# The PSUM bank of the transposes joined with the three of the channel mixing into one ring of four, with new order lists, in a fused sliding-window attention and channel-mix kernel

## The chip, the cores and the metric

The kernel runs on one core of one Trainium2 chip. The metric is the device time of one execution in microseconds (us), the median of several runs. Each order list below belongs to one engine of that core: PE (the matrix engine), DVE (the vector engine), ACT (the scalar engine), POOL and SP, which in this kernel mostly issue transfers.

## The reference

Attention over a sliding window of 128 tokens with a linear distance bias, for 8 batches, 8 heads, 576 tokens and head size 64, followed by a channel mix over the 512 joined head columns:

```python
scores = scale * np.matmul(q, k.transpose(0, 1, 3, 2))
bias = slopes[:, None, None] * (-np.abs(rel).astype(np.float32))[None, :, :]
mask = (rel >= 0) & (rel < window)              # rel = query - key, window = 128
scores = np.where(mask, scores + bias[None], -1000000000.0)
attn = softmax(scores)                          # over the keys
x = np.matmul(attn, v)                          # heads joined: (8, 576, 512)
xk = mu_k * x + (1.0 - mu_k) * x_prev           # x_prev: x one token earlier
xr = mu_r * x + (1.0 - mu_r) * x_prev
k = np.maximum(xk @ w_k, 0.0)                   # w_k: 512 x 1024
v = k * k @ w_v                                 # w_v: 1024 x 512
r = 1.0 / (1.0 + np.exp(-(xr @ w_r)))           # w_r: 512 x 512
return r * v
```

Inputs and output are float32; the kernel multiplies in bf16 and accumulates in float32.

## The kernel before

**Tiling.** The unit of the attention is a pair of heads of one batch: 32 pairs, numbered `it` = 0 to 31, four to a batch. The unit of the channel mix is two batches (1152 tokens) cut into chunks: four chunks for the first two batches, three (512, 384 and 256 tokens) for each later two. All of it is one program of small steps. A step is registered by `op(...)` with its engine, its inputs and the ring from which it takes a buffer.

**Steps of a pair.** `ct.it` (DVE) puts q and k of the pair in token order. `tq.it` (PE) transposes them into PSUM, and `pq.it` (ACT) copies them out. `score.it.h` (PE, halves h = 0 and 1) multiplies, `exp.it.h` (ACT) takes the exponential, `mask.it.h` (DVE) applies window and bias. `av.it` (PE) multiplies by v, `norm.it` (DVE) divides, `ot.it` (PE) transposes the result, `xt.it` (ACT) copies it out. `xk.it` and `xr.it` (DVE) mix it with the token before.

**Steps of a chunk**, for two batches P and a start column c0 or a row block c: `m1.P.c0.fo` (PE, product with w_k), `rl` (ACT, maximum with 0), `kk` (DVE or ACT, square), `m3.P.c` (PE, product with w_r), `rs.P.c` (ACT, gate), `m2a.P.c` and `m2.P.c` (PE, two halves of the product with w_v), `oo.P.c` (DVE, gate times value), `st.P.c` (SP, store).

**Loads.** POOL issues nearly all loads, one after the other: `lql.b...` (q and k of batches 0 to 3), `lvs.b.j` (v of batch b, five pieces; pairs 4b to 4b+3 need all of them), `lts.b.i` (the last 64 tokens of q and k), `lqn.b.i.j` (q and k of batches 4 to 7; i = 0 is q, i = 1 is k). A load also waits until the load eight issues earlier has landed.

**Batches 4 to 7** are not transposed on PE. SP issues a transposing transfer `tr.b.0` (q) and `tr.b.1` (k) from the loaded tile to `qt_buf`, and `trt.b.0`, `trt.b.1` for the last 64 tokens. There is a single `qt_buf`: the transfers of batch b must wait until all scores of batch b-1 have read it. The first half of a pair's scores needs both `tr`, the second half both `trt` as well. `lqn` of batch 6 overwrites the tile that the `tr` of batch 4 read, and `lqn` of batch 7 that of batch 5.

**PSUM.** The pools are opened in lines 65 to 67: `p_sa` (2 buffers of 2 banks: scores, and av from pair 4 on), `p_tp` (1 bank: all `tq` and `ot`), `p_mm` (3 banks: `m1`, `m3`, `m2a`/`m2`, and in the first batch the small products). A PE step that takes a buffer waits until the step that empties the previous content of that buffer is done: an ACT copy for `tq` and `ot`, `rl`, `rs` or `oo` for the others.

**Order.** A planner (`plan`) would choose the order by priorities, but the table `ORDER` fixes it: one list of step names for each engine, each engine runs its list from first to last, and a step that is not ready blocks everything behind it on that engine. The same holds for the loads in POOL's list and for the transfers in SP's.

Of the kernel before, what the change touches and what calls it, by code (L numbers as in the profile page):

```python
# [9 lines left out]
BF16 = mybir.dt.bfloat16  # L10
# [6 lines left out]
def kernel(  # L17
# [136 lines left out]
    def qk_transp(it, t0, t1, pool, tag):  # L154
        cs = T["cs", it]
        tp = T["tp", it, t0] = pool.tile([128, 1024], BF16, tag=tag, name="tp")
        for n in range(NF * t0, NF * t1):
            nc.tensor.transpose(  # L158
                tp[:, 128 * (n - NF * t0):128 * (n - NF * t0) + 128],
                cs[:, n // NF, n % NF].rearrange("p h d -> p (h d)"), ident)  # L160
# [105 lines left out]
    def x_transp(it, t0=0, t1=NJ):  # L266
        xu = T.pop(("xu", it, t0))
        tp = T["xt", it, 128 * t0] = p_tp.tile([128, 1024], BF16, tag="tp", name="tp")
        for t in range(t0, t1):
            nc.tensor.transpose(  # L270
                tp[:, 128 * t:128 * t + 128], xu[:, t].rearrange("p h d -> p (h d)"), ident)
# [177 lines left out]
    RINGS = {"sa": 2, "tp": 1, "mm": 3, "ct": 3, "xu": 3, "dl": 4, "xm": 3, "xk": 2, "rl": 3,  # L449
# [77 lines left out]
    def add_pair(it):  # L527
# [9 lines left out]
        if b == 0:  # L537
# [38 lines left out]
        else:  # L576
# [7 lines left out]
            op(("tq", it), "PE", 450, lambda: qk_transp(it, 0, 2, p_tp, "tp"), war, n, "tp",  # L584
# [17 lines left out]
        if b == 0:  # L602
            for e, (t0, t1) in enumerate(((0, 2), (2, NJ))):
# [6 lines left out]
                   [], n, "tp", uses=[("norm", it, e)])  # L610
# [22 lines left out]
        op(("ot", it), "PE", 290, lambda: x_transp(it), [], n, "tp", uses=[("norm", it)])  # L633
# [88 lines left out]
    for i, m in enumerate(FILL):  # L722
# [9 lines left out]
            m1.0.256.5 m1.0.256.4 tq.6 m1.0.256.7 av.4 score.6.0 m1.0.256.1 ot.4 av.5 score.6.1
            tq.7 m3.0.2 m3.0.1 m1.0.256.2 ot.5 score.7.1 score.7.0 tail.2 m1.0.0.7 m3.0.0 tq.8
            av.6 m3.0.3 av.7 tq.9 m2a.0.0 m2a.0.1 ot.6 score.8.1 score.8.0 m2a.0.3 ot.7 m2.0.0
            m2.0.1 score.9.1 score.9.0 m2.0.3 m1.0.512.0 tq.10 m1.0.512.4 m1.0.512.1 m1.0.512.2
            av.8 m1.0.512.5 m2a.0.2 score.10.1 score.10.0 m1.0.512.7 ot.8 m2.0.2 av.9 tq.11
            m1.0.512.6 m1.0.512.3 m3.0.4 score.11.1 score.11.0 m3.0.8 ot.9 m3.0.6 m3.0.5 tq.12
            m1.0.768.0 av.10 m1.0.768.1 tq.13 m1.0.768.2 m1.0.768.7 score.12.0 score.13.0 m2a.0.4
            tail.3 ot.10 av.11 m2.0.4 tq.14 score.12.1 m2a.0.5 score.14.1 tq.15 m2.0.5 score.13.1
            score.14.0 m1.0.768.3 ot.11 m1.0.768.5 av.12 m1.0.768.4 m1.0.768.6 score.15.0  # L740
            score.15.1 m3.0.7 ot.12 av.13 m1.1.0.0 av.14 score.17.0 m1.1.0.7 score.18.0 score.16.1
            m2a.0.6 score.18.1 m2.0.6 score.17.1 m2a.0.7 av.15 score.16.0 m1.1.0.5 ot.13
            score.19.1 score.19.0 m2a.0.8 m2.0.7 ot.14 m2.0.8 m3.1.1 ot.15 m1.1.0.1 m1.1.0.6
            m3.1.0 m3.1.2 m1.1.0.4 m3.1.3 av.17 m1.1.512.0 av.16 m1.1.0.2 m1.1.512.7 m1.1.0.3
            m1.1.512.4 m1.1.512.3 ot.16 av.18 av.19 m2a.1.2 m2a.1.3 ot.17 m2a.1.0 m2.1.2 m2.1.0
            m2.1.3 ot.18 m2a.1.1 score.21.1 score.20.0 ot.19 m2.1.1 score.22.1 m1.1.512.5
            m1.1.512.2 score.20.1 m3.1.4 m1.1.896.0 score.23.1 score.22.0 m3.1.6 m3.1.8 m1.1.512.6
            m1.1.512.1 score.21.0 score.23.0 m3.1.5 m1.1.896.2 m3.1.7 av.20 m2a.1.6 m1.1.896.6
            m2.1.6 ot.20 av.21 m1.1.896.4 m1.1.896.7 m2a.1.5 av.22 m2a.1.4 m2.1.5 ot.21 m2.1.4
            m1.1.896.3 m1.2.0.0 m1.1.896.1 m1.2.0.4 m1.2.0.1 m1.2.0.3 m1.1.896.5 m1.2.0.7 ot.22  # L750
            av.23 m3.2.0 m1.2.0.5 m1.2.0.2 m3.2.1 ot.23 m2a.1.8 m1.2.0.6 score.27.1 score.24.1
            m2.1.8 m3.2.2 score.25.0 score.26.0 m2a.1.7 m2a.2.0 score.26.1 score.25.1 m2.1.7
            m2a.2.1 score.24.0 score.27.0 m2.2.0 m2.2.1 m1.2.512.0 m3.2.3 m1.2.512.7 m1.2.512.6
            m1.2.512.5 m2a.2.3 av.24 m2a.2.2 m2.2.3 m3.2.6 m2.2.2 av.25 ot.24 m1.2.896.0 m3.2.4
            m1.2.512.2 m1.2.512.3 m1.2.512.4 av.26 m1.2.896.6 m1.2.896.7 m1.2.512.1 ot.25
# [6 lines left out]
            m1.3.512.7 m3.3.4 m3.3.8 m1.3.512.5 m1.3.512.4 m1.3.512.6 m1.3.512.3 m1.3.896.0 m3.3.7
            m1.3.896.7 m3.3.5 m1.3.896.2 m2a.3.5 m2a.3.4 m2.3.5 m2.3.4 m1.3.896.1 m3.3.6
            m1.3.896.3 m1.3.896.6 m1.3.896.5 m2a.3.6 m1.3.896.4 m2.3.6 m2a.3.8 m2.3.8 m2a.3.7
            m2.3.7
# [230 lines left out]
```

## Time and profile before

| what | value |
|---|---|
| time, median of 3 runs (lowest to highest) | 238.65 us (238.22 to 239.57) |
| span of the profiled execution, first to last instruction | 237.9 us |
| PE busy | 223.9 us (94%) |
| DVE busy | 193.2 us (81%) |
| ACT busy | 165.7 us (70%) |
| POOL busy | 93.2 us (39%) |
| mean granted clock of PE | 1.000 |

The profile gives the span of its own execution, and no device time for it. The three runs lie 0.3 to 1.7 us above that span, their median 0.75 us: this is what lies around the instructions. Busy time of PE counts each matmul from its start to its modelled end, so a matmul that streams in 216 ns may be listed with 380. DMA rows give the time from issue to landing.

### The profile page before, as it was taken

How to read it: one execution, taken by the hardware profiler on the slowest of the kernel's cores; microseconds unless marked ns; L12 is line 12 of the kernel's file. 1: busy time of each engine (PE TensorE's matmuls, PEld its weight loads, DVE VectorE, ACT ScalarE, POOL GpSimd, SP SyncE). 2: the span in 40 equal slices, each digit the busy share in tenths (PEclk: the TensorE clock that was granted, in tenths of full speed). 3: DMA queues.
4: the chain of work that ended last, by engine and by line, in shares of the span. 5: the costliest groups of instructions: out<-in, count | busy, mean ns of one | idle time of the engine just before them, and what ended most of it. 6: DMA issues, size and time to landing. Idle time of an engine off the chain costs nothing.

```text
span 237.9 us, 5426 instructions
## 1 busy us (share of the span) xinstructions
PE 223.9 (94%) x2130; PEld 132.9 (56%) x2163; DVE 193.2 (81%) x406; ACT 165.7 (70%) x281; POOL 93.2 (39%) x131
## 2 busy tenths in 40 slices
PE   6798888999999699999999999999999999999994
PEld 2355675757666465556455655445675455545573
DVE  3869999999979689998889897689669989993252
ACT  4397799978999789785299448875578974407340
POOL 8999567568646378407876610000000000000000
PEclk9999999999999999999999999999999999999999
DMA  6999999999999999999999999627220300203024
GB/s 131 166 137 184 178 160 200 188 159 210 202 139 149 134 164 135 125 123 212 193 171 184 123 123 181 193 77 148 99 90 3 118 19 0 91 0 132 0 91 178
DMA packets 114810, 31.56 MB, mean 133 GB/s; under 512 B 99160, under 2 KB 110432, under 8 KB 114784
## 3 DMA queue, kind: packets, MB, share of 16 engines
q0 software_dynamic: 89808, 16.52, 107.2%
q1 hardware_dynamic: 24976, 14.69, 29.7%
q8 instruction: 17, 0.28, 0.5%
q14 instruction: 9, 0.07, 0.1%
HBM read 33.56 MB, written 9.44 MB: 181 GB/s over the span
## 4 chain that ended last, share of the span: by engine, by line
PE 76%; DVE 13%; DMA 3%; ACT 3%; issue 2%; POOL 1%; POOLq 0%; DVEq 0%
PE pv L351 23%; PE ps L313 22%; PE pr L336 13%; PE sa L250 6%; PE sa L219 5%; PE tp L270 3%; DMA ql<-in_k_dram 3%; DVE at L232 2%; DVE xu L262 2%; DVE xk L302 2%; ACT at L227 2%; PE pv L358 1%; PE tp L158 1%; DVE ct L149 1%; DVE xr L302 1%
## 5 line engine op out<-in xcount | busy, mean ns | idle before, releaser
L313 PE MATMUL ps<-xk,wk_sb 128*128 128x256 bf16 (+2 forms) x410 | 71.9, 313 | 0.7 <-DVE xk L302 0.4
L319 ACT ACTIVATE rl<-ps 128x256 bf16<-128x256 f32 (+2 forms) x104 | 47.6, 476 | 31.1 <-PE ps L313 27.0
L227 ACT ACTIVATE at<-sa 128x1024 bf16<-128x1024 f32 x64 | 64.3, 1035 | 4.1 <-PE sa L219 3.9
L351 PE MATMUL pv<-wv_sb,kk 128*128 128x512 bf16 x257 | 63.9, 379 | 1.3 <-issue 0.6
L313 PEld LDWEIGHTS <-wk_sb 128*128 128x128 bf16 x416 | 38.7, 98 | 24.2 <-issue 2.0
L351 PEld LDWEIGHTS <-kk 128*128 128x128 bf16 x272 | 24.3, 98 | 24.3 <-issue 1.5
L232 DVE TENSOR_TENSOR at<-at,mask 128x1024 bf16<-128x1024 bf16 x56 | 37.5, 683 | 0.5 <-ACT at L227 0.2
L328 DVE TENSOR_TENSOR kk<-rl 128x256 bf16<-128x256 bf16 (+2 forms) x88 | 28.3, 335 | 10.7 <-ACT rl L319 10.1
L336 PE MATMUL pr<-wr_sb,xr 128*128 128x512 bf16 x135 | 35.6, 380 | 0.5
L366 DVE SCALAR_TENSOR_TENSOR ot<-rs,pv 128x512 f32<-128x512 bf16 (+1 forms) x38 | 24.5, 656 | 11.2 <-PE pv L351 4.9
L110 POOL DMA_DIRECT2D vs<-in_v_dram x32 | 28.6, 904 | 6.0 <-PE tp L270 2.4
L275 ACT COPY xt<-tp 128x576 bf16<-128x576 bf16 (+2 forms) x36 | 21.3, 590 | 13.4 <-PE tp L270 13.3
L302 DVE SCALAR_TENSOR_TENSOR xk<-dl,mu_sb,xt 128x576 bf16<-128x576 bf16 (+2 forms) x36 | 27.1, 752 | 1.3
L342 ACT ACTIVATE rs<-pr 128x512 bf16<-128x512 f32 x36 | 21.7, 611 | 8.8 <-PE pr L336 8.7
L302 DVE SCALAR_TENSOR_TENSOR xr<-dl,mu_sb,xt 128x576 bf16<-128x576 bf16 x32 | 25.5, 811 | 0.0
L250 PEld LDWEIGHTS <-at 128*128 128x128 bf16 x576 | 21.2, 98 | 6.4 <-issue 2.4
L262 DVE TENSOR_TENSOR xu<-sa,rc 128x640 bf16<-128x640 f32 x28 | 23.1, 824 | 1.0
L250 PE MATMUL sa<-vs,at 128*128 128x65 bf16 x448 | 18.9, 194 | 1.9 <-ACT rl L319 1.9
L336 PEld LDWEIGHTS <-xr 128*128 128x128 bf16 x144 | 13.4, 98 | 13.0 <-issue 0.6
L88 POOL DMA_DIRECT2D ql<-in_k_dram x16 | 14.2, 894 | 14.8 <-DMA qt<-ql 11.0
L138 ACT COPY qk<-tp 128x1024 bf16<-128x1024 bf16 (+1 forms) x16 | 14.7, 917 | 6.1 <-DVE qk L135 3.8
L295 DVE TENSOR_TENSOR dl<-xt 128x576 bf16<-128x576 bf16 (+2 forms) x36 | 15.1, 418 | 3.0 <-ACT xt L275 3.0
(70 smaller groups left out, 222.8 us busy)
## 6 DMA issues: line engine op xcount, KB each, us to landing
out_dram<-ot SPq DMA_DIRECT2D x34, 256.0 KB, 3.8
vs<-in_v_dram POOLq DMA_DIRECT2D x32, 128.0 KB, 9.8
ql<-in_k_dram POOLq DMA_DIRECT2D x17, 128.0 KB, 8.2
ql<-in_q_dram POOLq DMA_DIRECT2D x17, 128.0 KB, 7.3
ql<-in_q_dram POOLq DMA_DIRECT2D x7, 256.0 KB, 8.3
ql<-in_k_dram POOLq DMA_DIRECT2D x7, 256.0 KB, 7.6
wk_sb<-in_moe_w_k_dram POOLq DMA_DIRECT2D x2, 512.0 KB, 8.7
wv_sb<-in_moe_w_v_dram POOLq DMA_DIRECT2D x2, 512.0 KB, 10.2
```

Of the source, the lines that this page charges most:

```text
L110: nc.gpsimd.dma_start(out=vs_buf[b % NLD][:, j, :, 0:D], in_=v[b, :, 128 * j:128 * j + 128, :].rearrange("h p d -> p h d"))
L227: nc.scalar.activation(out=at_half(it, e), in_=T.pop(("sa", it, e)), func=AF.Exp, scale=float(scale))
L232: nc.vector.tensor_tensor(out=at_half(it, e), in0=at_half(it, e), in1=mask[:, 2 * g:2 * g + 2, 256 * e:256 * e + 512], op=ALU.mult)
L250: nc.tensor.matmul(pa[:, hl, W * (t - t0):W * (t - t0) + W], lhsT=at[:, lo:lo + 128], rhs=vs[:, u, 2 * g + hl, :] if u < NF else tvb[:, 2 ...
L262: nc.vector.tensor_tensor(out=xu[:, t0:t1].rearrange("p t h d -> p h t d"), in0=a5[:, :, :, 0:D], in1=rc[:, :, 0:n, None].to_broadcast([12 ...
L302: nc.vector.scalar_tensor_tensor(out=to, in0=T["dl", it][:, c0:c1], scalar=mu_sb[:, NPO * which + g:NPO * which + g + 1], in1=xp, op0=ALU. ...
L313: nc.tensor.matmul(ps[:, 0:c1 - c0], lhsT=wk_sb[:, po, 128 * fo:128 * fo + 128], rhs=xk[:, po, c0:c1], start=(po == 0), stop=(po == NPO - 1))
L319: nc.scalar.activation(out=rl[:, 0:c1 - c0], in_=T.pop(("ps", P, c0, fo))[:, 0:c1 - c0], func=AF.Relu, scale=RELU_SCALE)
L328: nc.vector.tensor_tensor(out=T["kk", P, c0][:, fo, 0:c1 - c0], in0=rl[:, 0:c1 - c0], in1=rl[:, 0:c1 - c0], op=ALU.mult)
L336: nc.tensor.matmul(pr, lhsT=T["xr", P][:, po, 128 * c:128 * c + 128], rhs=wr_sb[:, po], start=(po == 0), stop=(po == NPO - 1))
L351: nc.tensor.matmul(pv, lhsT=kk[:, fo, o:o + 128], rhs=wv_sb[:, fo], start=(fo == 0), stop=(fo == NFO - 1))
L366: nc.vector.scalar_tensor_tensor(out=T["ot", P, c][:, w0:w1], in0=T["rs", P, c][:, w0:w1], scalar=1.0, in1=pv[:, 0:w1 - w0], op0=ALU.add, ...
```

## The change

The pool `p_tp` is gone and `p_mm` has four buffers in place of three; all `tq` and `ot` now take their bank from `p_mm`. PSUM holds eight banks before and after. The work is the same: every list has the same step names, 375 on PE, 276 on ACT, 318 on DVE, 112 on POOL, 58 on SP. The order of each of the five lists is new from beginning to end.

```diff
     p_sa = ctx.enter_context(tc.tile_pool(name="p_sa", bufs=2, space=bass.MemoryType.PSUM))
-    p_tp = ctx.enter_context(tc.tile_pool(name="p_tp", bufs=1, space=bass.MemoryType.PSUM))
-    p_mm = ctx.enter_context(tc.tile_pool(name="p_mm", bufs=3, space=bass.MemoryType.PSUM))
+    p_mm = ctx.enter_context(tc.tile_pool(name="p_mm", bufs=4, space=bass.MemoryType.PSUM))
...
-        tp = T["tp", it, t0] = pool.tile([128, 1024], BF16, tag=tag, name="tp")
+        tp = T["tp", it, t0] = p_mm.tile([128, 1024], BF16, tag="mm", name="tp")
...
-        tp = T["xt", it, 128 * t0] = p_tp.tile([128, 1024], BF16, tag="tp", name="tp")
+        tp = T["xt", it, 128 * t0] = p_mm.tile([128, 1024], BF16, tag="mm", name="tp")
...
-    RINGS = {"sa": 2, "tp": 1, "mm": 3, "ct": 3, "xu": 3, "dl": 4, "xm": 3, "xk": 2, "rl": 3,
+    RINGS = {"sa": 2, "mm": 4, "ct": 3, "xu": 3, "dl": 4, "xm": 3, "xk": 2, "rl": 3,
...
-            op(("tq", it), "PE", 450, lambda: qk_transp(it, 0, 2, p_tp, "tp"), war, n, "tp",
+            op(("tq", it), "PE", 450, lambda: qk_transp(it, 0, 2), war, n, "mm",
...
         "SP": """
-            lq.0.0 lmu.0 lq.0.1 lmu.1 st.0.1 st.0.3 st.0.2 tr.4.0 st.0.0 tr.4.1 trt.4.0 trt.4.1
+            lq.0.0 lq.0.1 lmu.0 lmu.1 tr.4.0 st.0.1 st.0.0 tr.4.1 trt.4.0 st.0.3
```

Three places of the new order matter below. In the rows, `vs` is v (`vs_90` and `vs_87` hold batch 3), `ql` is the tile of q and k, `ts` the last 64 tokens, `qt` and `tt` what the transposing transfers write. `DMASW` is the wait for the load eight issues earlier, `DMAHW` a wait for a transfer of SP.

POOL before, from the last two pieces of v of batch 3 (`lvs.3.1`, `lvs.3.0`) on:

```order
L110 DMA vs_90<-in_v_dram 128x8x64 [waits DMASW1_49]
L110 DMA vs_90<-in_v_dram 128x8x64 [waits DMASW2_49]
L110 DMA vs_91<-in_v_dram 128x8x64 [waits DMASW3_49,PE_49]
L124 DMA ts_96<-in_q_dram 64x8x64 [waits DMASW4_49,PE_49]
L88 DMA ql_94<-in_k_dram 128x8x64 [waits DMASW5_49,DVE_49]
L88 DMA ql_94<-in_k_dram 128x8x64 [waits DMASW6_49,DVE_49]
L88 DMA ql_94<-in_k_dram 128x8x64 [waits DMASW7_49]
L124 DMA ts_98<-in_k_dram 64x8x64 [waits DMASW0_49]
L110 DMA vs_92<-in_v_dram 128x8x64 [waits DMASW1_49,PE_49]
L88 DMA ql_94<-in_k_dram 128x8x64 [waits DMASW2_49]
L88 DMA ql_93<-in_q_dram 128x8x64 [waits DMAHW7_49,DMASW3_49]
```

The last row is `lqn.6.0.0`, the first load of batch 6; its `DMAHW7` is `tr.4.0`. POOL after, at the same place (`lts.4.0`, `lqn.4.1.0`, `lvs.3.0`, `lqn.6.1.3`, `lvs.4.3`, `lqn.5.0.0` and on):

```order
L123 DMA ts_94<-in_q_dram 64x8x64 [waits DMASW1_49]
L87 DMA ql_90<-in_k_dram 128x8x64 [waits DMASW2_49]
L109 DMA vs_87<-in_v_dram 128x8x64 [waits DMASW3_49]
L87 DMA ql_90<-in_k_dram 128x8x64 [waits DMAHW7_49,DMASW4_49]
L109 DMA vs_88<-in_v_dram 128x8x64 [waits DMASW5_49,PE_49]
L87 DMA ql_91<-in_q_dram 128x8x64 [waits DMASW6_49,DVE_49]
L87 DMA ql_91<-in_q_dram 128x8x64 [waits DMASW7_49,DVE_49]
```

The last load of batch 4's k (`lqn.4.1.0`) has moved from eleven issues ahead of `lvs.3.0` to one ahead of it, and a load of batch 6 stands right behind `lvs.3.0`, ahead of every load of batch 5 and of v of batch 4. Its `DMAHW7` is now `tr.4.1`.

SP before, at the transposing transfers of batch 5 (`trt.5.1`, `tr.5.1`, `tr.5.0`, a store, `trt.5.0`):

```order
L98 DMA_TRANSPOSE tt_104<-ts_98 128x4x64 [waits DMAHW5_49,DMASW0_49,PE_49]
L93 DMA_TRANSPOSE qt<-ql_94 128x16x128 [waits DMASW6_49,DMASW7_49,DMASW5_49,DMAHW1_49,DMASW3_49,DMAHW6_49,DMASW2_49,PE_49]
L93 DMA_TRANSPOSE qt<-ql_94 128x16x128 [waits DMASW7_49,DMASW2_49,DMAHW7_49,DMASW1_49,DMASW0_49]
L371 DMA out_dram<-ot 128x512 [waits DMAHW0_49,DVE_49]
L98 DMA_TRANSPOSE tt_104<-ts_98 128x4x64 [waits DMASW5_49]
```

SP after (`tr.5.0`, a store, `trt.5.1`, `tr.5.1`, `trt.5.0`):

```order
L92 DMA_TRANSPOSE qt<-ql_91 128x16x128 [waits DMASW6_49,DMASW7_49,DMASW4_49,DMAHW6_49,DMASW1_49,PE_49]
L370 DMA out_dram<-ot 128x512 [waits DMAHW7_49]
L97 DMA_TRANSPOSE tt_101<-ts_95 128x4x64 [waits DMAHW0_49,DMASW5_49]
L92 DMA_TRANSPOSE qt<-ql_91 128x16x128 [waits DMASW5_49,DMASW3_49,DMAHW1_49,DMASW1_49,DMASW0_49]
L97 DMA_TRANSPOSE tt_101<-ts_95 128x4x64 [waits DMAHW2_49,DMASW2_49]
```

The two large transposing transfers stood together and stand apart now, with a store and the other small transfer between them; the `PE_49` on the first large one is the wait for the last score of batch 4 in both lists. On PE, the steps between that score (`score.19.0`) and the first score of batch 5 (`score.21.1`), which needs all four transfers, were 10 `m2a`/`m2`, 4 `m3`, 9 `m1` (5 of 512 columns, 4 of 384), 4 `av` and 5 `ot`; now they are 5 `m2a`/`m2`, 2 `m3`, 11 `m1` (4 of 512, 7 of 384), 3 `av` and 2 `ot`.

More of the change, by code (lines that the diff above doesn't have):

```diff
@@ L732 @@
[L732 to L743, printed above, removed]
@@ L762 @@
[L762 to L765, printed above, removed]
+            fill.0 fill.1 tk.0 tq.0 score.0.0 tmu tq.3 tail.0 tq.2 score.0.1 score.2.0
+            tq.1 score.2.1 av.0.0 av.2.0 score.3.0 ot.0.0 ot.2.0 av.0.1 av.2.1
+            score.1.0 score.1.1 av.3.0 ot.0.1 ot.2.1 av.1.0 score.3.1 av.1.1 ot.3.0
@@ new lines @@
+            m2a.0.1 m2a.0.0 score.9.0 score.10.1 ot.7 m2.0.1 m2a.0.3 m2.0.0 m2.0.3
+            m1.0.512.0 score.9.1 score.10.0 m1.0.512.5 tail.3 tq.11 m1.0.512.4
+            m1.0.512.7 m2a.0.2 av.8 m2.0.2 m1.0.512.3 m1.0.768.0 ot.8 m1.0.768.1
+            score.11.1 score.11.0 tq.12 m1.0.512.6 m3.0.6 av.9 m1.0.512.1 m1.0.768.2
+            m3.0.4 ot.9 score.12.1 score.12.0 tq.13 m1.0.768.6 m3.0.5 m3.0.8 av.10
+            tq.14 av.11 m1.0.768.7 m1.0.512.2 score.13.0 score.13.1 m1.0.768.3 ot.10
@@ new lines @@
+            m3.0.7 m1.0.768.5 m2a.0.5 score.14.1 score.14.0 ot.11 m1.0.768.4 m2.0.5
+            av.12 m2a.0.4 av.13 m2.0.4 tq.15 ot.12 m2a.0.8 score.15.0 score.17.0
+            m2a.0.6 m1.1.0.0 av.14 m2.0.6 score.15.1 score.18.0 m2.0.8 m1.1.0.6
+            score.18.1 score.16.1 m2a.0.7 ot.14 m2.0.7 ot.13 score.16.0 score.17.1
+            m1.1.0.5 m1.1.0.7 av.15 m3.1.3 m3.1.0 score.19.1 score.19.0 ot.15 m1.1.0.3
+            m3.1.1 m1.1.0.4 m1.1.0.1 m1.1.0.2 m1.1.512.0 m3.1.2 av.16 m1.1.512.5
@@ new lines @@
+            mask.9.0 kk.0.768.0 kk.0.512.3 ct.15 ct.13 norm.9 mask.10.1 mask.11.0
+            kk.0.512.6 kk.0.768.2 ct.14 xk.8 mask.11.1 norm.10 norm.11 mask.12.1
+            kk.0.768.6 kk.0.512.2 kk.0.768.7 mask.12.0 xk.9 mask.13.1 xk.10 kk.0.768.3
+            xr.9 mask.13.0 oo.0.5 norm.12 mask.14.1 norm.13 oo.0.4 xk.11 mask.14.0
+            kk.0.768.4 mask.15.0 norm.14 xr.10 mask.15.1 oo.0.8 oo.0.6 mask.18.0
+            kk.1.0.0 xr.8 mask.16.1 oo.0.7 mask.18.1 xr.11 xk.12 kk.1.0.6 norm.15
@@ new lines @@
+            kk.1.0.7 xk.14 xk.13 mask.17.1 xk.15 mask.16.0 kk.1.0.3 xr.12 kk.1.0.2
+            kk.1.0.4 norm.16 mask.17.0 mask.19.1 kk.1.512.0 xr.13 xr.15 oo.1.0
+            kk.1.512.4 oo.1.2 kk.1.512.3 norm.18 norm.17 kk.1.512.6 xr.14 oo.1.3
+            kk.1.512.2 mask.19.0 mask.22.1 xk.16 norm.19 oo.1.1 kk.1.512.7 mask.21.0
+            xk.18 mask.22.0 kk.1.896.0 xk.17 kk.1.896.2 mask.20.1 xk.19 mask.23.0
+            kk.1.896.7 xr.16 mask.20.0 mask.23.1 oo.1.6 norm.22 oo.1.4 xr.17 oo.1.5
```

220 lines of the change are left out of this document (114 added, 106 removed).

## Prediction

> **What bounds the kernel now.** I read the page first, then the windows for the stage in which PE (matrix engine) loses time, then PE's waits, then the timeline around the largest of them. The page and four windows (the stretch, then busy us of PE, weight loads, DVE, ACT and POOL):
>
> ```profile
> span 237.9 us, 5426 instructions
> ...
> 20.00:30.00 10.00, 8.89 (x112) 6.28 (x110) 9.58 (x31) 7.50 (x17) 7.11 (x10) 1.00 1.64 181
> 30.00:40.00 10.00, 8.29 (x120) 6.45 (x120) 9.93 (x24) 9.59 (x17) 6.81 (x9) 1.00 1.79 175
> ...
> 80.00:90.00 10.00, 8.07 (x108) 5.13 (x111) 7.25 (x15) 7.66 (x12) 7.16 (x9) 1.00 2.22 159
> ...
> 200.00:210.00 10.00, 9.95 (x82) 5.37 (x80) 9.13 (x18) 3.60 (x6) 0.00 (x0) 1.00 0.14 54
> ```
>
> Between 20 and 40 us DVE is full and PE idles 2.8 us; at 80 PE idles once more, 1.9 us; later it is full. PE's waits from 35 to 90 us and from 90 to 230 us, the longest row of each:
>
> ```profile
> PE sa L250 <- ACT rl L319: 1.9, 1, 1.9
> ```
>
> ```profile
> PE pv L351 <- issue: 0.3, 2, 0.2
> ```
>
> So after about 82 us nothing holds PE up. The place itself, in the timelines of PE, DVE and POOL, and the landing times of v loads issued between 60 and 68 us (shortest, median, longest):
>
> ```profile
> 79.16 0.81 PE L313 MATMUL ps<-xk,wk_sb 128*128 128x384 bf16 x4
> 81.83 0.62 PE L250 MATMUL sa<-vs,at 128*128 128x65 bf16 x15 [1.85 <-ACT rl L319]
> ```
>
> ```profile
> 79.83 0.68 DVE L232 TENSOR_TENSOR at<-at,mask 128x1024 bf16<-128x1024 bf16 x1
> ```
>
> ```profile
> 65.20 1.77 POOL L110 DMA_DIRECT2D vs<-in_v_dram  x2
> ```
>
> ```profile
> DMA to landing us min/median/max: 10.3/14.0/15.6
> ```
>
> The waiting step is `av.12`. It needs no `rl`, and the DVE row shown is the last mask before `norm.12`, done at 80.5; but it is the first reader of v of batch 3, whose last piece `lvs.3.0` is the second of the two loads at 65.20, issued at 66.1. With 15.6 us it lands at 81.7. A load, not ACT, ends that wait: PE was free at 79.98.
>
> **The anchor.** `av.12` stands behind the same amount of matrix work in both lists. Rates from the chain of waits (start, us, matmuls):
>
> ```profile
> 42.18 0.55 PE sa L219 x12
> ...
> 44.35 0.45 PE tp L158 x8
> 44.80 0.55 PE sa L250 x18
> ...
> 47.20 1.73 PE pv L351 x8
> ...
> 82.54 1.30 PE ps L313 x8
> ...
> 85.36 0.28 PE tp L270 x5
> ```
>
> A 512-column matmul streams in 0.216 us, four make 0.864; four of 384 make 0.65; a `tq` costs 0.45, an `av` 0.55, an `ot` 0.28, the two halves of a score 0.55. Ahead of `av.12` only `m2a.0.4`, `m2.0.4` and `tq.15` have left (2.18) and `m1.0.768.4`, `m1.0.768.6`, `m3.0.7` have come (2.16). What follows is therefore the same too, and it was free of waits: the span is the start of `av.12` plus 237.9 - 81.8 = 156.1 us plus new waits behind it. The run's time adds 0.75 us (median 238.65 less span).
>
> **The change, part by part.**
>
> *The ring itself: 0.* PE's waits hold no row in which a `tq` or `ot` waits for the ACT copy that empties the single bank, so nothing is removed. Added: any matrix product may now wait for the copy four allocations back. The nearest row, PE's whole wait for ACT's q/k copies,
>
> ```profile
> PE sa L219 <- ACT qk L138: 1.3, 2, 0.6
> ```
>
> bounds this at 1.3 us either way; with no bank wait in the trace I take 0. The Trainium skill, page "TensorE: Matmul & The Clock Gate", section "HAM oscillation — how this bites in real kernels", reports a kernel in which more PSUM buffers gave no further gain. The trace agrees so far that no bank wait shows; by that rule the time would stay at 238.65.
>
> *The start of `av.12`: -2.3.* Up to there PE follows DVE, which is full. DVE's list ahead of `norm.12` loses a mask, an `oo` and an `xr` and gains two `kk` and an `xr`:
>
> ```profile
> 72.01 0.62 DVE L328 TENSOR_TENSOR kk<-rl 128x384 bf16<-128x384 bf16 x2
> ...
> 77.42 1.89 DVE L232 TENSOR_TENSOR at<-at,mask 128x1024 bf16<-128x1024 bf16 x3
> 79.23 0.68 DVE L366 SCALAR_TENSOR_TENSOR ot<-rs,pv 128x512 f32<-128x512 bf16 x1
> ```
>
> That is 0.63 + 0.60 - 0.62 = 0.6 us less, so PE would come at 79.4, give or take 1 for the reordered first 20 us. The load sets the other condition. `lqn.4.1.3` must wait for `ct.11`, which has 3.7 us more DVE work ahead than before (out `xr.4`; in `ct.10`, one `kk`, `oo.0.1`, two `xk`, `xr.5`):
>
> ```profile
> 49.19 0.89 DVE L149 COPY ct<-ql 128x1024 bf16<-128x1024 bf16 x2
> ```
>
> ```profile
> 52.08 3.52 POOL L88 DMA_DIRECT2D ql<-in_k_dram  x4 [0.57 <-DMA vs<-in_v_dram]
> ```
>
> `ct.11` was the first of that pair and ended at 49.6; now 53.3. From `lqn.4.1.3` (52.08) to `lvs.3.0` (66.1) 14 issues took 14.0 us. Now there are 15, the first eight into an emptied queue at 0.88 each (3.52 for four): 53.3 + 7.0 + 7.0 = 67.3. Landing takes 10.3 to 15.6, so 77.6 to 82.9; both large transfers of batch 4 ran into the old one (below), now one does, so I take 11.7: 79.0. `av.12` starts at 79.5 instead of 81.8; bounds 78.4 and 82.9.
>
> *`tr.4.1` before `score.17.0`: +0.8.* SP's rows and the landing of its transfers (issues from 57 to 62 us and from 158 on, then the small ones from 108 on):
>
> ```profile
> 61.87 5.51 SPq L93 DMA_TRANSPOSE qt<-ql  x1
> ...
> 68.17 6.95 SPq L93 DMA_TRANSPOSE qt<-ql  x1
> ...
> 95.70 11.63 SPq L93 DMA_TRANSPOSE qt<-ql  x2
> ...
> 108.01 1.19 SPq L98 DMA_TRANSPOSE tt<-ts  x1
> ...
> 158.47 4.49 SPq L93 DMA_TRANSPOSE qt<-ql  x2
> ```
>
> ```profile
> qt<-ql SPq DMA_TRANSPOSE x1, 12.9
> ```
>
> ```profile
> qt<-ql SPq DMA_TRANSPOSE x2, 4.8
> ```
>
> ```profile
> tt<-ts SPq DMA_TRANSPOSE x2, 7.6
> ```
>
> Before, `tr.4.1` was issued at 68.17 and landed at 81.1, 6 us early. Now its last load is the one ahead of `lvs.3.0`: issued at 66.4, landed after 10.3 to 14 us, at 76.7 to 80.4; say 77.5. The transfer takes 12.9 among loads and 4.8 without. POOL stands blocked behind `lvs.3.0` until it lands, so I take 7.5, nearer the row without: 85.0. PE comes at 79.5 + 0.55 + 4.15 (three half products, `av.13`, `tq.15`, `ot.12`, half a score) = 84.2. It waits 0.8; bounds 0 and 9. Queued behind it is all of PE.
>
> *`trt.4.1` before `score.18.1`: +0.3.* It follows on SP at about 84 and lands in 7.6, at 91; PE, 5.7 us of work later, comes at 90.7. Bounds 0 and 3.
>
> *Batch 5 before `score.21.1`: +1.6.* `score.19.0` ends 13.7 us of work after `score.17.0`: 85.0 + 0.3 + 13.7 = 99.0. Before, the last of the four transfers landed 108.01 + 7.6 - 95.70 = 19.9 us after that score, hidden by 22.6 us of PE work (19 times 0.864, 4 times 0.65, 4 `av`, 5 `ot`). Now 16.2 us stand there (11 times 0.864, 7 times 0.65, 3 `av`, 2 `ot`) and one small transfer more is in the queue: 21.1 us. At these prices PE waits 4.9. But the second large transfer would run after POOL's queue has emptied, at the price of the pair at 158 (2.2 to issue each), and then it waits not at all. I take a third of the upper end.
>
> *Batch 6: +0.3.* Its loads stand behind `lqn.7.1.3`, which waits for `tr.5.1` as the old list's first load of batch 7 did:
>
> ```profile
> 108.66 0.88 POOL L88 DMA_DIRECT2D ql<-in_k_dram  x1 [11.03 <-DMA qt<-ql]
> ```
>
> Before, PE showed no wait for batch 6; now 15 loads at about 1 us and a landing of 8 us follow `tr.5.1` before the last can start. Bounds 0 and 4.
>
> The sum: -2.3 + 0.8 + 0.3 + 1.6 + 0.3 = +0.7: a span of 238.6, a time of 239.4 us.
>
> **The rivals.** (1) The gates stay open: the transfers run at their price without loads, and only the first term counts: 238.65 - 2.3 = 236.4. For it: the 4.8 row; against: loads are still landing when each transfer starts. (2) Slower: the four transfers of batch 5 keep the old prices (19.9 plus 1.2 us) against 16.2 us of PE work, and PE stands 4.9 us before `score.21.1`; with the other terms 239.4 + 3.3 = 242.7. It decides from the point where that chain exceeds 16.2 us. For it: in the old trace the second transfer, too, took 5.8 us to issue after POOL had stopped; against: there loads were still landing. (3) The change does nothing: PE's stalls are of loads and DVE, which a bank cannot shorten, and the new order only shifts them: 238.65.
>
> **How the numbers follow.** Half a per cent, 1.2 us, is about what a measurement of this kernel can tell from no change. Forecast 0.38, its own range 237.4 to 241.4 (a tenth of it faster, half the same, four tenths slower); rival 1 0.29 (nearly all faster); rival 2 0.23 (slower); rival 3 0.10 (mostly the same). Faster: 0.04 + 0.25 + 0.02 = 0.31; the same 0.30; slower 0.39. The low end is `av.12` at 78.4 with no wait behind, 238.65 - 3.4 = 235.2; the high end rival 2 with 1.3 more from the bounds of `tr.4.1`, 244.0.
>
> **What would show it.** Right: PE idles less between 20 and 82 us, `av.12` starts near 79.5, and short PE waits stand at the first scores of batches 4 and 5 (near 84 and 115), released by transposing transfers. Wrong: no PE wait over 0.5 us there (rival 1), or one near 5 us at batch 5 (rival 2); `av.12` no earlier than 81.8, or waits of PE for `qk`, `xt` or `rs` copies, would break the first two terms.

## The result, and the profile after

Four executions took 235.38 us in the median (235.28 to 237.92), against 239.11 us (238.22 to 240.52) for four of the kernel before on the same chip: a ratio of 0.9873, 95% interval 0.9828 to 0.9918. A second series, with sixteen executions of before, gave 0.982 (0.978 to 0.9859). By the two series the change saves 1.3 and 1.8 per cent, 3 to 4.3 us. Ratios are of undisturbed executions alone, so they can differ by some tenths of a per cent from the quotient of two medians.

The page and the windows of the changed kernel (stretch, then busy us of PE, weight loads, DVE, ACT and POOL):

```profile
span 233.5 us, 5421 instructions
...
20.00:30.00 10.00, 8.28 (x116) 5.58 (x114) 9.69 (x26) 9.60 (x16) 5.87 (x9) 1.00 1.69 185
30.00:40.00 10.00, 9.03 (x121) 7.47 (x122) 8.77 (x24) 8.45 (x19) 6.48 (x9) 1.00 1.91 163
80.00:90.00 10.00, 9.89 (x98) 5.17 (x98) 8.72 (x16) 6.84 (x9) 9.20 (x11) 1.00 1.94 157
```

The hole at 80 is gone (9.89 where 8.07 stood). From 35 to 90 us PE's waits have no row at all; from 90 to 230 the longest is

```profile
PE pv L350 <- issue: 0.3, 2, 0.2
```

So none of the waits on transposing transfers that the sum counted is there. `av.12` in the timeline of PE:

```profile
77.02 1.03 PE L350 MATMUL pv<-wv_sb,kk 128*128 128x512 bf16 x4
77.88 0.62 PE L249 MATMUL sa<-vs,at 128*128 128x65 bf16 x15
```

It starts at 77.88 without a wait, 3.95 us earlier than before; behind it stand 233.5 - 77.88 = 155.6 us, where 156.1 stood. The loads and transfers around it: POOL's issue of `lvs.3.0` and the next one, SP's two large transfers of batch 4, and the landing of the loads and of the transfers (those issued from 65 to 68, then from 71 to 76):

```profile
66.31 0.91 POOL L109 DMA_DIRECT2D vs<-in_v_dram  x1
78.87 0.88 POOL L87 DMA_DIRECT2D ql<-in_k_dram  x1 [11.66 <-DMA qt<-ql]
```

```profile
66.78 4.16 SPq L92 DMA_TRANSPOSE qt<-ql  x1
...
73.18 3.20 SPq L92 DMA_TRANSPOSE qt<-ql  x1
```

```profile
ql<-in_k_dram POOLq DMA_DIRECT2D x1, 128.0 KB, 5.5
vs<-in_v_dram POOLq DMA_DIRECT2D x1, 128.0 KB, 7.8
...
qt<-ql SPq DMA_TRANSPOSE x1, 8.3
```

```profile
qt<-ql SPq DMA_TRANSPOSE x1, 5.2
```

`lvs.3.0` was issued within 1 us of the estimate but landed at 66.31 + 7.8 = 74.1, not 79.0. The last load that `tr.4.1` needs (`lqn.4.1.0`, the `ql` row) landed 5.5 us after its issue at 65.43, not 10.3 to 14, so the transfer was issued at 73.18, not at 77.5, and landed at 73.18 + 5.2 = 78.4, not 85.0. `score.17.0`, and the first score of batch 5 behind its transfers:

```profile
82.65 0.38 PE L218 MATMUL sa<-qt 64*128 64x256 bf16 x4
...
113.25 0.34 PE L218 MATMUL sa<-qt 64*128 64x256 bf16 x4
```

```profile
97.00 1.58 SPq L92 DMA_TRANSPOSE qt<-ql  x1
...
101.40 1.80 SPq L92 DMA_TRANSPOSE qt<-ql  x1
103.29 1.71 SPq L97 DMA_TRANSPOSE tt<-ts  x1
```

```profile
qt<-ql SPq DMA_TRANSPOSE x2, 4.3
tt<-ts SPq DMA_TRANSPOSE x2, 2.3
```

Landing is counted from the issue. So the last two of the four transfers of batch 5 land at 101.40 + 4.3 = 105.7 and about 103.29 + 2.3 = 105.6 (the last one has no landing of its own in the trace; 2.3 is that of the other small one). That is 8.7 us behind 97.00, where 21.1 were feared, and 7.5 us early. In both places POOL issues no further load while the transfers run; at batch 5 its next load stands until `tr.5.1` has landed:

```profile
106.24 0.88 POOL L87 DMA_DIRECT2D ql<-in_k_dram  x1 [12.66 <-DMA qt<-ql]
```

Batch 6 is another case: its second large transfer, issued at 133.9, took 12.9 us among loads and landed at 146.8, and the first score that reads it starts at 148.88. Nothing waited, with 2 us to spare.

One correction to the base: the executions of this study lie 1.7 to 1.95 us above their own spans (235.28 for 233.5). The profiled execution of before, 237.9 us, was therefore most likely the one of 239.57, the slowest of three, and the 0.75 us that the prediction added should have been about 1.75.

### The profile page after: what moved, and what is told of

Its sections match the earlier page's. It is cut to its first block, busy times and chain, and to the rows that moved or that the text cites. A ratio compares the mean times of both kernels' runs of the same rounds, so it can differ in the third digit from the quotient of the medians.

```text
span 233.5 us, 5421 instructions
## 1 busy us (share of the span) xinstructions
PE 222.2 (95%) x2130; PEld 132.7 (57%) x2163; DVE 192.6 (82%) x406; ACT 163.7 (70%) x281; POOL 93.1 (40%) x131
## 4 chain that ended last, share of the span: by engine, by line
PE 83%; POOL 9%; DMA 5%; issue 1%; ACT 0%; DVE 0%; POOLq 0%
PE ps L312 25%; PE pv L350 25%; PE pr L335 13%; PE sa L249 7%; PE sa L218 6%; DMA vs<-in_v_dram 5%; PE tp L269 4%; POOL vs L109 2%; POOL ql L129 2%; PE tp L157 2%; PE pv L357 2%; POOL ts L123 1%; POOL tv L440 1%; POOL wk_sb L422 1%; POOL ql L118 1%
## 5 line engine op out<-in xcount | busy, mean ns | idle before, releaser
L312 PE MATMUL ps<-xk,wk_sb 128*128 128x256 bf16 (+2 forms) x415 | 73.0, 314 | 0.7 <-DVE xk L301 0.3
L226 ACT ACTIVATE at<-sa 128x1024 bf16<-128x1024 f32 x64 | 65.7, 1051 | 7.5 <-PE sa L218 7.4
L350 PEld LDWEIGHTS <-kk 128*128 128x128 bf16 x272 | 25.1, 98 | 24.8 <-issue 0.8
L327 DVE TENSOR_TENSOR kk<-rl 128x256 bf16<-128x256 bf16 (+2 forms) x88 | 27.6, 335 | 8.9 <-ACT rl L318 8.7
L109 POOL DMA_DIRECT2D vs<-in_v_dram x32 | 29.3, 925 | 6.9 <-DMA wv_sb<-in_moe_w_v_dram 4.3
L341 ACT ACTIVATE rs<-pr 128x512 bf16<-128x512 f32 x36 | 22.3, 630 | 4.9 <-PE pr L335 4.8
L249 PEld LDWEIGHTS <-at 128*128 128x128 bf16 x576 | 21.5, 98 | 6.4 <-issue 1.1
```

What stands on the lines that cost most here:

```text
L109: nc.gpsimd.dma_start(out=vs_buf[b % NLD][:, j, :, 0:D], in_=v[b, :, 128 * j:128 * j + 128, :].rearrange("h p d -> p h d"))
L226: nc.scalar.activation(out=at_half(it, e), in_=T.pop(("sa", it, e)), func=AF.Exp, scale=float(scale))
L249: nc.tensor.matmul(pa[:, hl, W * (t - t0):W * (t - t0) + W], lhsT=at[:, lo:lo + 128], rhs=vs[:, u, 2 * g + hl, :] if u < NF else tvb[:, 2 ...
L312: nc.tensor.matmul(ps[:, 0:c1 - c0], lhsT=wk_sb[:, po, 128 * fo:128 * fo + 128], rhs=xk[:, po, c0:c1], start=(po == 0), stop=(po == NPO - 1))
L327: nc.vector.tensor_tensor(out=T["kk", P, c0][:, fo, 0:c1 - c0], in0=rl[:, 0:c1 - c0], in1=rl[:, 0:c1 - c0], op=ALU.mult)
L350: nc.tensor.matmul(pv, lhsT=kk[:, fo, o:o + 128], rhs=wv_sb[:, fo], start=(fo == 0), stop=(fo == NFO - 1))
```

## The experiments

### What slows the transposing transfers and `lvs.3.0`

**POOL runs on** (the changed kernel, POOL's list):

```diff
- lvs.3.0 lqn.6.1.3 lvs.4.3 lqn.5.0.0 ... lqn.5.1.0 lts.5.0 lqn.6.1.2
+ lvs.3.0 lvs.4.3 lqn.5.0.0 ... lqn.5.1.0 lts.5.0 lqn.6.1.3 lqn.6.1.2
```

> The changed kernel, with lqn.6.1.3 (the load that stops POOL behind lvs.3.0 until tr.4.1 has landed) put behind the loads of batches 4 and 5 (behind lts.5.0), so that these are issued while tr.4.0 and tr.4.1 run. Theory (the price of a transposing transfer is set by the loads that land with it): tr.4.0 and tr.4.1 land in 11 to 13 us instead of 4 to 5, score.17.0 waits 3 to 5 us for tr.4.1 and score.18.1 up to 1 more for trt.4.1, time 235.4 + 3 to 6 = 238.4 to 241.4. Rival (the transfers are short for another reason, such as the bank ring or their place in SP's list): they stay at 4 to 6 us, no wait of PE over 0.5 us, 235.4.

Measured: 242.48 us, ratio 1.011 (1.0074 to 1.0146) to before, some 7 us more than the changed kernel. PE's waits from 35 to 90 us, SP's issue of `tr.4.1` and its landing, and `score.17.0`:

```profile
PE sa L218 <- DMA qt<-ql: 5.0, 1, 5.0
```

```profile
73.03 6.54 SPq L92 DMA_TRANSPOSE qt<-ql  x1
```

```profile
qt<-ql SPq DMA_TRANSPOSE x1, 14.5
```

```profile
87.62 0.61 PE L218 MATMUL sa<-qt 64*128 64x256 bf16 x4 [4.97 <-DMA qt<-ql]
```

Issued at the same time as in the changed kernel (73.03 and 73.18), the same transfer lands after 14.5 us instead of 5.2, and `tr.4.0` after 11.8 instead of 8.3, with loads landing beside them. The theory holds: for batch 4 the stopped POOL is what makes the new gate harmless. But it is not what lets `lvs.3.0` land early. Issued at 65.04 here, with other loads right behind it, that load landed after 5.9 us:

```profile
vs<-in_v_dram POOLq DMA_DIRECT2D x1, 128.0 KB, 5.9
```

So what brings it from 15.6 us in before to 7.8 and 5.9 stays open. In these two kernels `tr.4.0` is issued just behind it (66.78 and 65.95), in before 4 us ahead of it (61.87); that would fit theory B of the next run, but no run tests it alone. The price was above the range, for a reason in the windows behind the wait (the column behind the brackets is the granted clock):

```profile
88.00:90.00 2.00, 1.78 (x8) 0.74 (x6) 0.00 (x0) 1.02 (x1) 0.90 (x2) 0.50 1.38 208
90.00:92.00 2.00, 2.00 (x24) 1.04 (x22) 0.01 (x1) 0.00 (x0) 0.87 (x1) 0.77 1.87 231
```

After 5 us of idling PE was granted half its clock: 0.50 in the trace from 87.6 to 90.9 us, 0.98 from 90.9 to 91.5. From `score.17.0` to the end it takes 240.0 - 87.62 = 152.4 us, where the changed kernel takes 233.5 - 82.65 = 150.9. A wait of 5.0 us cost 6.5. This trace is of an execution of 241.81 us with a mean granted clock of 0.993; in ten of the other eleven the mean is 0.976 to 0.986 and the time 242.31 to 242.99 us. The Trainium skill, page "TensorE: Matmul & The Clock Gate", section "HAM oscillation — how this bites in real kernels", warns of PE gaps above about 3.4 us. The trace agrees: 0.50 behind this gap, and 1.00 at 80 to 90 us of before, with its gap of 1.85; where between these two the limit lies, no run here shows.

**POOL stopped in the kernel before** (its POOL list):

```diff
- lvs.3.1 lvs.3.0 lvs.4.2 lts.6.0
+ lvs.3.1 lvs.3.0 lqn.6.1.3 lvs.4.2 lts.6.0
```

> The kernel before, with one load of batch 6 (lqn.6.1.3, which waits for tr.4.1) put directly behind lvs.3.0 in POOL's list, so that POOL issues nothing until tr.4.1 has landed. Theory A (the loads issued behind lvs.3.0 are what slow it and the transposing transfers): lvs.3.0 lands 3 us or more earlier, av.12 starts when PE is free, at 80.0 instead of 81.8, tr.4.1 lands in under 9 us instead of 12.4, and the time is 238.65 - 1.85 = 236.8. Theory B (it is tr.4.0, started at 61.9 while loads are landing, that slows them): av.12 stays at 81 to 82, the wait stays near 1.8 us and the time at 238.6.

Measured: ratio 1.0066 (1.0024 to 1.0107), a little slower. The v loads issued from 64 to 66 us, POOL's next issue, `av.12`, and two later waits:

```profile
vs<-in_v_dram POOLq DMA_DIRECT2D x2, 128.0 KB, 10.5
```

```profile
79.43 0.88 POOL L88 DMA_DIRECT2D ql<-in_k_dram  x1 [13.42 <-DMA qt<-ql]
```

```profile
80.43 0.62 PE L250 MATMUL sa<-vs,at 128*128 128x65 bf16 x15
...
104.09 0.40 PE L250 MATMUL sa<-vs,at 128*128 128x65 bf16 x8 [0.42 <-DMA vs<-in_v_dram]
105.31 0.28 PE L250 MATMUL sa<-vs,at 128*128 128x65 bf16 x4 [0.82 <-DMA vs<-in_v_dram]
```

The load lands at about 75.7, 6 us earlier, and its wait is gone, as theory A said; but see the next two kernels. And `tr.4.1`, issued at 68.6, lands only at 79.4, when POOL goes on: 10.8 us, not under 9. A likely reason, not tested, is that `tr.4.0` still started among the loads at 62.5. And the v loads of batch 4 now come late, for 1.2 us of waits. In these two kernels a stop paid where the transfers stand behind the last load and nothing behind it is urgent, and not otherwise.

**The first transfer later, and the load earlier** (the kernel before; SP's list, then POOL's, each a kernel of its own):

```diff
- tr.4.0 st.0.0 tr.4.1 trt.4.0
+ st.0.0 tr.4.1 tr.4.0 trt.4.0
```

> The kernel before, with tr.4.0 put behind tr.4.1 in SP's list, so that the first transposing transfer starts at 68 us, not at 61.9 (tr.4.1 waits for lqn.4.1.0 and was issued at 68.2). Theory B (a transposing transfer among loads slows the loads): loads issued between 60 and 68 us land in about 7 us as in the changed kernel instead of 14, av.12 starts at 80.0, time 236.8; tr.4.0 then lands near 85, ahead of score.17.0. Theory A (the loads issued behind lvs.3.0 slow it): av.12 at 81 to 82, time 238.6.

```diff
- lvs.3.2 lts.4.1 lvs.3.4 lvs.3.1 lvs.3.0
+ lvs.3.2 lvs.3.0 lts.4.1 lvs.3.4 lvs.3.1
```

> The kernel before, with lvs.3.0 issued three loads earlier (behind lvs.3.2). It tests the anchor of the prediction. Anchor right: av.12 finds its load landed, starts at 80.0 instead of 81.8, and the whole of the 1.85 us comes out at the end: 236.8. Anchor wrong (another thing is late next, or the tail is not rigid): 238.2 or more.

Measured: ratios 1.0 (0.9961 to 1.0039) and 1.0011 (0.9975 to 1.0047). In the first, `tr.4.1` could already start at 64.05, so it moved the transfer by only 2 us and tells little of theory B. The v loads issued from 60 to 68 us landed after 8.2 to 11.0 us in its trace, and after 8.3 to 10.6 in the other's, though POOL is not stopped by a transfer in either, so the 10.5 us above do not show that the stop shortened the load. In the second, `av.12` waits for nothing and still starts no earlier:

```profile
81.55 0.62 PE L250 MATMUL sa<-vs,at 128*128 128x65 bf16 x15
```

237.6 - 81.55 = 156.05: the tail is as rigid as the anchor said, but PE itself came 1.6 us later than in the profiled execution of before. Removing a wait of 1.85 us is worth nothing in an execution in which PE is late anyway. Of these 1.6 us 0.7 were lost at the first load, ahead of anything that its edit moves. DVE's timeline of this kernel, of before and of the changed kernel:

```profile
6.77 0.66 DVE L135 CAST cs<-ldr 128x512 bf16<-128x512 f32 x1 [2.83 <-DMA ldr<-in_k_dram]
```

```profile
6.05 0.55 DVE L135 CAST cs<-ldr 128x512 bf16<-128x512 f32 x1 [2.05 <-DMA ldr<-in_k_dram]
```

```profile
2.71 1.24 DVE L408 TENSOR_SCALAR sid<-ident 128x128 bf16<-128x128 bf16 x8
3.62 0.59 DVE L134 CAST cs<-ldr 128x512 bf16<-128x512 f32 x1
4.13 0.68 DVE L405 COPY dist<-dist 128x256 bf16<-128x256 bf16 x3
4.69 0.41 DVE L134 CAST cs<-ldr 128x512 bf16<-128x512 f32 x1
```

The old list idles for the second half of the first load, 2 to 3 us; the new one has `sid` and `dcopy` there and does not wait.

### Ring, compute lists, load lists

Each of these takes a part of the change alone. Old lists cannot simply be put on the new ring: `ot.7` would need a bank that only `m2.0.0`, later in PE's list, lets go. Each kernel has the few moves that this asks for.

**Ring alone** (old lists on four banks: `m2.0.0` before `ot.7`, and three like it).

> The lists of before with the ring of four banks; four steps are moved so that no step waits for a bank that a later one frees (m2.0.0 ahead of ot.7 on PE, oo.0.0 ahead of xk.7 on DVE, xt.19 and xt.21 a few places earlier on ACT). Theory (the ring itself is worth nothing, the lists hold the gain): 238.65 give or take 1.3, av.12 waits for lvs.3.0 as before. Rival (the shared banks free PE by themselves): 237.4 or less, with less idle time of PE between 0 and 40 us.

**Lists alone** (new lists on one bank and three: `pk.3` before `pk.2`, and five like it).

> The new lists with the old pools, one bank for the transposes and three for the products; six steps are moved so that nothing waits for a bank that a later step frees (pk.3, xt.0.1, xt.3.0, xt.14, xt.27 earlier, m2.2.6 earlier). Theory (the lists hold the gain): 235.4 to 236.6, av.12 near 78. Rival (the lists need the fourth bank): 237.9 or more, with waits of PE for a qk or xt copy at the transposes that stand close together.

**Load lists alone** (POOL's list and the places of SP's transfers from the new kernel, all else old).

> The kernel before with POOL's list of the changed kernel, and SP's transfers in its places (the stores in the order in which the old DVE list makes them). Theory: lvs.3.0 lands well before PE, av.12 starts at 80.0, the transfers of batch 4 land in about 5 us, no wait over 0.5 us behind it: 236.8, that is half of the gain; the other half needs the new start. Rival (loads and transfers change nothing by themselves): 238.6.

**Compute lists alone** (the reverse, on the new ring).

> The changed kernel with POOL's list of before, and SP's transfers in the places of before (the stores in the order in which the new DVE list makes them). Theory (the loads' and transfers' lists carry most of the gain): PE comes to av.12 at 78, but lvs.3.0 lands at about 81 as before, and the transfers of batch 5 keep 12 us each against 16 us of PE work: 238.5 to 243. Rival (the new PE, ACT and DVE lists carry it): 235.4 to 236.6.

Measured, as ratios to before: ring alone 1.0026 (0.9986 to 1.0067); lists alone 1.0824 (1.0765 to 1.0884); load lists alone 0.9968 (0.9938 to 0.9998), 0.8 us; compute lists alone 1.1301 (1.1241 to 1.1361). The ring by itself is worth nothing, but the theory that the lists hold the gain without it falls: on the old banks they take 19 us more than before, 23 more than the changed kernel, in PE's waits over the whole run

```profile
PE tp L270 <- ACT xt L275: 5.9, 6, 1.9
...
PE tp L158 <- ACT qk L138: 2.0, 2, 1.1
...
PE tp L158 <- ACT xt L275: 1.9, 4, 0.8
```

and others like them: transposes that stand close together wait for the copy that empties the one bank. The load lists alone gain less than half of the 1.85 us that their theory had: the large transfers issued from 68 to 71 us land fast and `av.12` has no wait, but PE is no earlier:

```profile
qt<-ql SPq DMA_TRANSPOSE x2, 6.2
```

```profile
80.63 0.62 PE L250 MATMUL sa<-vs,at 128*128 128x65 bf16 x15
```

The compute lists alone do far worse than either theory had it, because the lists interlock: a `tail` waits 13.2 us for a load that stands elsewhere in the old POOL list, and `score.17.0` waits 10.1 us for a transposing transfer.

```profile
PE to L170 <- DMA ts<-in_q_dram: 13.2, 1, 13.2
PE sa L218 <- DMA qt<-ql: 10.1, 1, 10.1
```

### Where the compute lists gain

**New start** (steps of the old PE, ACT and DVE lists up to `tq.9`, `pq.9` and `ct.9` put into the new order, the rest old): with new loads, with old loads, and with new loads on the old banks.

> Ring of four banks, the new lists of POOL and SP, and the old lists of PE, ACT and DVE in which only the first part (up to tq.9, pq.9 and ct.9, about the first 42 us) is put into the new lists' order. Theory (the compute lists gain only at the start): PE comes to av.12 at 78 to 78.8 as in the changed kernel, no wait over 0.5 us behind it, 235.4 to 236.2. Rival (the gain is spread over the whole lists): av.12 at 79.5 or later, 237 or more.

> The same kernel with POOL's and SP's lists of before. Theory (the start brings PE early, the load lvs.3.0 then stops it): PE comes to av.12 at 78 to 79 and waits 2 to 3 us for lvs.3.0, which lands at 81 among loads and transfers as before; time 237.5 to 238.6. Rival (the start alone is enough): 235.4 to 236.2.

> New loads, new start, but one bank for the transposes and three for the products (nine steps moved so that nothing waits for a bank that a later step frees). Theory (the new start needs the shared banks, since tq, ot and tail stand close together in it): PE waits at transposes for qk and xt copies, several us in the first 42 us, 238 or more. Rival (the start's gain is of DVE's and the loads' order alone): 235.4 to 236.5.

Measured: 1.0048 (1.0023 to 1.0072), 1.0283 (1.024 to 1.0326), 1.0482 (1.044 to 1.0523). The first is on the rival's side, but slower than before, which neither had; the second misses both; the third is as its theory said. The first has waits of its own where the lists are joined, from 40 to 60 us,

```profile
PE tp L269 <- DVE tt L176: 1.9, 1, 1.9
PE pr L335 <- ACT qk L137: 1.4, 1, 1.4
```

so its time doesn't show what the start is worth. In the second PE waits 6.2 us for one `ct`, whose load stands elsewhere in the old POOL list. The third against the first says again that the new start needs the shared banks.

**First loads undone** (the changed kernel):

```diff
- SP: lq.0.0 lq.0.1 lmu.0 lmu.1      POOL: clear0 lql.0.1.0 lql.0.1.1
+ SP: lq.0.0 lmu.0 lq.0.1 lmu.1      POOL: lql.0.1.0 lql.0.1.1 clear0
```

> The changed kernel, in which only the first loads have the old order: lmu.0 between lq.0.0 and lq.0.1 on SP, and POOL's first two loads ahead of its memsets (clear0). Theory (a part of the start's gain is that the second half of the first q and k no longer lands late): lq.0.1 lands 1 to 2.5 us later, c.0.1 and tk.0 wait for it, and the whole delay comes out at the end: 236.4 to 237.4. Rival (sid and dcopy, now ahead of c.0.1 on DVE, cover it): 235.4, within 0.5 us.

Measured: 235.74 us, ratio 0.9821 (0.9783 to 0.9859). In its trace PE's first transposes are 1.45 us later (7.32 for 5.87) and `av.12` 0.4 (78.28 for 77.88), no more than two traces of the changed kernel differ (77.88 and 78.54). The rival is right: most of it is swallowed.

**DVE work added** to the changed kernel, early and late (`pad` is a scratch tile of the same shape), and the base again:

```diff
+ for i in range(2):
+     op(("pad", i), "DVE", 900, lambda: nc.vector.tensor_copy(out=pad, in_=mask[:, 0:H, 0:224]), [("mcopy", 0)], 0)
  DVE: ... xk.2.0 pad.0 pad.1 norm.3.0 ...      or      ... norm.16 pad.0 pad.1 mask.17.0 ...
```

> The changed kernel with two needless DVE copies (128x1792, bf16, into a scratch tile) behind xk.2.0, at about 19 us. The 128x2048 copy of the masks took 0.92 us in the changed kernel, so two of 128x1792 take 1.4 to 1.6 us. Theory (DVE is the bound from 16 to 35 us, and its lost time there comes out at the end one for one): av.12 at 79.3 to 79.5, time 235.4 + 1.4 to 1.6 = 236.8 to 237.0. Rival (the start has slack, as in the run with the first loads undone, where 1.0 of 1.45 us was swallowed): 235.4 to 236.0.

> The changed kernel with the same two copies behind norm.16, at about 100 us, where DVE is 90% busy but PE is full. Theory (PE bounds from 40 us on, so that DVE time is free there): 235.4 within 0.5 us. Rival (DVE bounds there too): 236.8 to 237.0.

> The changed kernel once more, beside the three others on the same chip. Both theories: 235.4, av.12 at 77.7 to 78.3, span at 156 us behind it.

Measured: 235.81 (235.22 to 236.51), 235.26 (234.84 to 235.56) and 235.12 us (234.27 to 236.18). The copies took 0.69 and 0.62 us (early), 1.31 together. Late they cost nothing. Early they cost about 0.7 in the median, with ranges that overlap: in the rival's range, and half of the one for one that the theory had. In the profiled execution of the base DVE waited for a load at the same place,

```profile
20.13 1.17 DVE L148 COPY ct<-ql 128x1024 bf16<-128x1024 bf16 x2 [1.03 <-DMA ql<-in_k_dram]
```

and such a wait can take up added work; in the first trace of the changed kernel it is 0.2 us. So the start seems to be held by DVE and by loads in turn, which is argued from two traces.

**Old start filled** (the kernel before; DVE's `id8 c.0.0 c.0.1 sid dcopy` becomes `id8 sid c.0.0 dcopy c.0.1`, SP's and POOL's first loads as in the changed kernel, `lvs.3.0` three loads earlier).

> The kernel before, old rings, with four moves: sid and dcopy go ahead of c.0.0 and c.0.1 on DVE (they fill its waits for the first q and k), lq.0.1 ahead of lmu.0 on SP, clear0 ahead of POOL's first loads, and lvs.3.0 three loads earlier. Theory (DVE's idle time in the first 24 us sets when PE comes to av.12): DVE idles 4 us there instead of 6.2 to 7.8, PE comes to av.12 at 79.5 or earlier and finds its load landed, 236.5 to 237.5. Rival (another wait of the start, such as PE's for ct, takes its place): av.12 at 80.5 or later, 238.2 or more.

Measured: 238.97 us, ratio 0.9971 (0.9941 to 1.0). Four moves without the ring gain 0.3 per cent, 0.6 at the most: the rival's case. Filling those 2 us of DVE's idle time is not by itself what the new start gains. Its one trace is of an execution of 246.08 us, too far from the median to show what took the rest.

### What the traces say together

PE's arrival at `av.12`, by its own row less any wait: with the old compute lists 79.98, 80.43, 81.51, 81.55, 80.37 and 80.63 (before, POOL stopped, transfer late, load early, ring alone, load lists alone), 80.75 on average; with the new ones 77.88, 77.72, 78.28, 77.68 and 78.54 (after, POOL runs on, first loads undone, late copies, base again), 78.02 on average. From the start of `av.12` to the end it is 156.05 to 156.1 us in the four old ones without a later wait and 155.6 to 155.7 in the four new ones. So the new compute lists bring PE 2.7 us earlier and save 0.4 behind; with 0 to 1.85 us of the load's wait, that makes 3.1 to 5, around the measured 3 to 4.3 us.

The traces also show when PE gets ahead. `av.1.0` is the 26th step of PE's list before and after, and 23 of the 25 steps ahead of it are the same (before has `tail.1` and `score.3.1` besides, after `ot.2.1` and `fill.1`). Its rows, before and after:

```profile
21.17 0.36 PE L250 MATMUL pa<-vs,at 128*128 128x65 bf16 x6
```

```profile
18.74 0.35 PE L249 MATMUL pa<-vs,at 128*128 128x65 bf16 x6
```

In the six traces with the old compute lists listed above it starts at 20.28 to 22.77 (21.5 on average), in the five with the new ones at 18.28 to 19.48 (18.8). With the new start it comes at 18.73 on the new loads and at 19.38 on the old, but at 21.59 on the old banks; the new lists on the old banks have 21.84. The two pairs of steps differ by about 0.5 us of work, an estimate from rows like theirs. So most of PE's lead is made in the first 20 us, by the new order on the shared banks, and with either load list.

## Why the prediction was wrong

It forecast 239.4 us, with 0.39 on slower and 0.31 on faster, and gave this forecast a range of 237.4 to 241.4; the time is 235.38 us, just above the lowest value that it named at all (235.2, `av.12` early and no wait behind). The span was forecast at 238.6 and is 233.5, 5.1 us less: 3.0 from the gates, 1.65 from the start of `av.12`, 0.45 from the tail. The 0.75 us between span and time hid 1.0 of it.

- **The anchor** was right: the tail is rigid to 0.5 us. But its starting point came from one execution, in which PE was early (79.98) and the load late (81.7); in others of the same compute lists PE came at 80.4 to 81.6.
- **The ring itself: 0** was right (ratio 1.0026 alone). The Trainium skill, page "TensorE: Matmul & The Clock Gate", section "HAM oscillation — how this bites in real kernels", reports a kernel in which more PSUM buffers gave no further gain. The run of the ring alone agrees; taken as a rule for the whole change it would have left the time at 238.65, and that is not what came. For the lists that gain need the shared banks (23 us more without them). That use of the ring, allowing an order, the prediction did not weigh.
- **The start of `av.12`: -2.3** had the sign and not the size: -3.95. PE was put at 79.4 from 0.6 us less DVE work, "give or take 1 for the reordered first 20 us", and came at 77.9; the load was put at 79.0 and landed at 74.1 (after 7.8 us, not 11.7, and POOL's stop is not the reason). Most of the difference was made in those 20 us (`av.1.0` at 18.74 for 21.17). DVE's idle time there was in the trace (2.05 us for one load) and was not read, though the runs show that filling it is not the whole of the gain.
- **`tr.4.1`, `trt.4.1`, batch 5, batch 6: +0.8, +0.3, +1.6, +0.3** is the step that failed: all are 0. The text saw that POOL stands blocked, and still took 7.5 us for `tr.4.1`, between the rows with and without loads, and let it start at 77.5, behind a load that was to land after 10.3 to 14 us. That load landed after 5.5 us (5.9 with POOL running on), so `tr.4.1` was issued at 73.18 in either case (73.03). And the wait that it named as a new gate is also what empties the loads' queue: `tr.4.1` took 5.2, and batch 5's large ones 4.3. Taking the stop away brought 14.5 us and a wait of 5.0, which is the forecast's mechanism at its old price. For batch 6 the price stayed (12.9 us among loads); there PE's work hid it. The old price itself was read from the wrong row: the 12.9 us are those of `tr.4.0`, issued at 61.87, and the trace of before has no landing for `tr.4.1`, so the landing at 81.1, "6 us early", was not shown.
- **Rival 1** (gates open, 236.4) is what happened, with a larger start term. **Rival 2**'s wait at batch 5 never came; with POOL running on, a wait of its size came one batch earlier, at `score.17.0`. **Rival 3** is wrong for the whole and right for the ring alone.
- **Left open:** which of the moved steps of the first 20 us bring PE most of its 2.7 us. They need the shared banks and not the new loads; the times of the hybrids don't say more, since these stalled behind their joints, and neither the first loads nor DVE time alone accounts for it.

## What to carry to other kernels

Price a transfer by what lands beside it in the new order, not by its row in the old one: here a load placed so that it must wait for the transfer stopped POOL's whole list and let the transfer run alone. A wait read from one trace is worth what the next latest condition leaves of it, and PE's arrival moved by 1.6 us (79.98 to 81.55) between traces with the same compute lists. A resource that shows no wait can still be worth something if it makes another order possible; test it with that order, not alone.

## What the runs showed of the hardware

The same 128 x 2048 transposing transfer landed after 4.3 to 5.2 us with no loads issued beside it, after 8.3 where the last loads were still landing when it started, and after 10.8 to 14.5 among loads; in before, v loads issued beside them landed after 10.3 to 15.6 us, the last one of the changed kernel, behind which POOL stops, after 7.8, and after 5.9 where POOL ran on. After a wait of 5.0 us PE was granted 0.50 of its clock for 3.3 us, and the rest of the run took 1.5 us longer. The time of an execution lay 1.7 to 1.95 us above its span.
